# Moving a 2 MB weight load behind the LN2 transposes and fixing ScalarE's and VectorE's order in a two-branch mixer kernel

## Chip, cores, metric

One core of one Trainium2 chip. The metric is the device time of one execution in microseconds (us). Profile times count from the start of the span; the time of a run is about 1.7 us longer than its span (290.91 for a span of 289.2). "Granted clock" is the share of full TensorE clock that the profile records. The record is a list of stretches at 1.00 or 0.50. The mean granted clock also counts a drop in the last microseconds, after the last matmul (from 287.92 in the kernel before).

## The reference

For x of 2048 x 640 (bf16), the output is g * a + (1 - g) * b. Here a is a linear-attention block, g a sigmoid gate per row, and b an MLP with token shifts:

```python
h   = gelu(layernorm(x) @ w1)                  # LN1, W1
hs  = shifted(h) @ w2                          # four column groups, shifted by 1, -1, 2, -2 tokens
x1  = x + hs                                   # W2 and residual
h2  = gelu(layernorm(x1) @ w3) @ w4            # LN2, W3 (640x1728), W4 (1728x640)
b   = x1 + h2
```

## The kernel before

The rows are worked in 4 tiles of 512 rows, each of 4 chunks (`cc`) of 128. TensorE (PE) needs the normalised rows transposed. So ScalarE (ACT) writes a normalised chunk into an `ln` buffer, of which there are three, and a DMA issued on the SP queue transposes it from there into `lnxT`. PSUM is four pairs of banks (`pair()`): a PE unit can start only when an earlier reader has emptied a pair. PE works its units in program order. ScalarE's and VectorE's (DVE) orders are fixed up to the end of W1 tile 1 and left to a scheduler after that.

```python
work = ctx.enter_context(tc.tile_pool(name="work", bufs=3))        # the ln buffers
ps = ctx.enter_context(tc.tile_pool(name="ps", bufs=4, space=PSUM))
# ... cut ...
    def ln1_apply(t, ccs=range(CPT)):
        # ... cut ...
            lnx = work.tile([P, D], BF16, name="ln")
            nc.scalar.activation(lnx[:], x_sb[:, c, :], ACT.Identity, bias=nb1[:, c:c + 1], scale=rstd1[:, c:c + 1])
            nc.sync.dma_start_transpose(lnxT[t][:, :, cc * P:(cc + 1) * P], lnx[:])
# ... cut: end of the first block, whose orders of PE, DVE and ACT are fixed ...
        for fcs in w1_split:
            w1_unit(0, fcs)
        ln1_apply(2)
        for gs in ((0, 1), (2, 3), (4, 5)):
            kv_unit(gs)
        for i, fcs in enumerate(w1_split):
            w1_unit(1, fcs)            # W1 matmuls, then their GELUs on ScalarE
            scale_unit(i)              # a small matmul, then pqT *= PSUM on VectorE
            ln1_apply(3, (i,))
        ln1_apply(3, (3,))

    w4_sb = area.tile([P, FC, D], BF16, tag="a")       # takes the place of the QKV weights
    nc.gpsimd.dma_start(w4_sb[:, 0:FC - 1, :], B_w4[0:(FC - 1) * P, :].rearrange("(c p) f -> p c f", p=P))
    # ... cut: memset and the last 64 rows of w4 ...
    def w2_unit(t, cc):
        # ... cut: 10 matmuls; x1 = PSUM + x and its statistics on VectorE; rstd, nb on POOL ...
        ln = work.tile([P, D], BF16, name="ln")
        nc.scalar.activation(ln[:], x1[:], ACT.Identity, bias=nb[:], scale=rstd[:])
        nc.sync.dma_start_transpose(st[t]["lnT"][:, :, cc * P:(cc + 1) * P], ln[:])
        nc.vector.tensor_scalar_mul(x1[:], x1[:], omg[:, c:c + 1])      # x1 *= 1 - g
# ... cut ...
    with tc.manual_schedule(engines={mybir.EngineType.PE}):
        for cc in range(CPT):
            w2_unit(0, cc)
        for i in range(2 * len(w1_split)):
            w1_unit(2 + i // 3, w1_split[i % 3])
            scale_unit(3 + i)
        scale_unit(9)
        for t in range(NT):
            # ... cut: W3, the next tile's W2, m_unit for t == 0, then W4 ...
```

## Time and profile before

| | before |
|---|---|
| timed runs, median | 293.77 us (292.96 to 294.78) |
| the profiled run: time, span | 290.91 us, 289.2 us |
| PE busy | 272.0 us, 94% of the span |
| mean granted clock | 0.980 |
| PE holes over 1.5 us | 7.87 us and 2.46 us |

From the page of the kernel before: busy tenths of PE and granted clock in 40 slices of 7.2 us.

```profile
span 289.2 us, 4297 instructions
...
PE   6999999999993596999999999999999999999994
...
PEclk9999999999999589999999999999999999999999
```

PE is full except in slices 13, 14 and 16 (and the first and last), and the clock is low in slices 14 and 15. The question is thus what PE waits for there. The table of PE's waits (us in total, times, longest):

```profile
PE pp L348 <- ACT hsT L390: 10.3, 2, 7.9
```

The timeline (start, duration, engine, line, operation; in brackets the idle time before and what ended it) shows the first hole from ScalarE's side:

```profile
83.40 1.38 POOL L448 DMA_DIRECT2D w_sb<-in_B_w_dram  x1 [4.82 <-ACT ln L373]
...
85.75 0.92 ACT L373 ACTIVATE ln<-x_sb,nb,rstd 128x640 bf16<-128x640 bf16 x1 [1.06 <-DMA lnxT<-ln]
...
95.45 0.92 ACT L373 ACTIVATE ln<-x_sb,nb,rstd 128x640 bf16<-128x640 bf16 x1 [8.30 <-DMA lnxT<-ln]
96.27 1.07 ACT L390 ACTIVATE hsT<-pp 128x512 bf16<-128x512 f32 x2
...
97.39 0.61 PE L348 MATMUL pp<-r_bf,emat 32*128 32x512 bf16 x2 [7.87 <-ACT hsT L390]
```

POOL issues the w4 load at 83.40. ScalarE's LN1 of tile 3 (L373 at 95.45) then waits 8.30 us for an `ln` buffer, which a transpose still holds. Behind it in ScalarE's order stands a GELU (L390), and behind that PE's scale matmul (L348). The DMA issues of the window 83 to 98 us (KB each, median us from issue to landing) say why the transposes are late:

```profile
w_sb<-in_B_w_dram POOLq DMA_DIRECT2D x1, 2080.0 KB, 11.4
lnxT<-ln SPq DMA_TRANSPOSE x5, 10.2
```

And PE's own timeline of this stretch, with the second hole:

```profile
97.93 8.37 PE L465 MATMUL pp<-w_sb,hsT 128*128 128x320 bf16 x40
...
115.12 0.39 PE L348 MATMUL pp<-r_bf,emat 32*128 32x512 bf16 x2 [2.46 <-ACT hsT L390]
...
117.03 2.33 PE L382 MATMUL pp<-lnxT,w_sb 128*128 128x512 bf16 x10
...
122.21 2.33 PE L490 MATMUL pp<-lnxT,w_sb 128*128 128x512 bf16 x10
```

W2 of tile 0 (L465, 40 matmuls) takes 8.37 us; elsewhere ten such take about 1.36 us, so 5.4 us would do. The granted clock is why. These are windows of 1 us (window, length, busy us of PE, PEld, DVE, ACT, POOL, granted clock, DMA share, GB/s):

```profile
92.00:93.00 1.00, 0.00 (x0) 0.00 (x0) 0.00 (x0) 0.00 (x0) 0.00 (x0) 1.00 1.15 140
93.00:94.00 1.00, 0.00 (x0) 0.00 (x0) 0.00 (x0) 0.00 (x0) 0.00 (x0) 0.68 1.06 194
...
103.00:104.00 1.00, 1.00 (x7) 0.64 (x6) 0.52 (x1) 0.00 (x0) 0.00 (x0) 0.70 0.27 52
104.00:105.00 1.00, 1.00 (x9) 0.73 (x8) 1.00 (x4) 0.00 (x0) 0.32 (x2) 1.00 0.00 0
```

PE stops at 89.52. The trace's clock record gives half clock from 93.36, thus 3.84 us later (the prediction read about 3.5 from these windows), and full clock again from 103.60.

### The profile page before, as it was taken

The page shows a single profiled execution, that of the slowest core. Times are in us where ns is not written, and L with a number is a line of the kernel's source. Part 1 is how long each engine was busy: PE and PEld are TensorE (multiplying, and loading weights), DVE is VectorE, ACT ScalarE, POOL GpSimd, SP SyncE. Part 2 cuts the span into 40 slices and gives each one's busy share as a digit, 9 for nine tenths or more (in the row PEclk, how much of TensorE's full clock was granted, in tenths as well). Part 3 has the DMA queues.
Part 4 walks back from the last instruction along what each step waited for, and adds up shares of the span by engine and source line. Part 5 has one row for each costly group of instructions (what it writes and reads, how often), then busy time and mean ns, then how long its engine had stood idle before and what let it go on. Part 6 is the DMA issues. An engine that isn't in the chain of part 4 may idle for free.

```text
span 289.2 us, 4297 instructions
## 1 busy us (share of the span) xinstructions
PE 272.0 (94%) x1740; PEld 161.6 (56%) x1740; DVE 131.7 (46%) x261; ACT 98.0 (34%) x121; POOL 37.9 (13%) x95
## 2 busy tenths in 40 slices
PE   6999999999993596999999999999999999999994
PEld 3776444667451252355467755477655577545773
DVE  1798777996954277856105136032244033100121
ACT  1455445244770716435521025411044401144000
POOL 8501000042230023011101002101012010000000
PEclk9999999999999589999999999999999999999999
DMA  7999870219329522102101101101002201100001
GB/s 231 219 306 357 217 297 0 39 31 133 66 41 308 98 57 56 23 2 45 24 2 44 48 23 32 38 22 46 25 23 45 25 24 48 45 0 2 23 25 44
DMA packets 41563, 22.66 MB, mean 78 GB/s; under 512 B 32406, under 2 KB 40471, under 8 KB 41543
## 3 DMA queue, kind: packets, MB, share of 16 engines
q1 hardware_dynamic: 40391, 19.36, 27.2%
q0 software_dynamic: 464, 2.21, 2.5%
q10 hardware_dynamic: 688, 0.82, 0.8%
q8 instruction: 13, 0.21, 0.3%
q14 instruction: 7, 0.06, 0.1%
HBM read 11.96 MB, written 2.62 MB: 50 GB/s over the span
## 4 chain that ended last, share of the span: by engine, by line
PE 82%; DMA 5%; ACT 4%; DVE 4%; POOL 3%; issue 1%; DVEq 0%; SPq 0%; ACTq 0%; POOLq 0%
PE pp L503 21%; PE pp L490 18%; PE pp L297 8%; PE pp L209 8%; PE pp L500 8%; PE pp L222 7%; PE pp L465 6%; DMA lnxT<-ln 4%; PE pp L382 3%; ACT ln L479 2%; POOL rstd L173 1%; DMA x_sb<-in_A_x_dram 1%; DVE x L469 1%; ACT ln L373 1%; PE pp L385 1%
## 5 line engine op out<-in xcount | busy, mean ns | idle before, releaser
L503 PE MATMUL pp<-w_sb,h 128*128 128x320 bf16 x448 | 66.1, 299 | 0.0
L490 PE MATMUL pp<-lnxT,w_sb 128*128 128x512 bf16 x280 | 63.2, 379 | 0.0
L503 PEld LDWEIGHTS <-h 128*128 128x128 bf16 x448 | 43.8, 98 | 17.0
L508 DVE SCALAR_TENSOR_TENSOR oc<-pp,omg,x 128x640 bf16<-128x640 f32 x15 | 13.2, 882 | 80.9 <-PE pp L503 80.9
L492 ACT ACTIVATE h<-pp 128x1024 bf16<-128x1024 f32 x28 | 28.6, 1021 | 61.7 <-PE pp L490 61.7
L490 PEld LDWEIGHTS <-w_sb 128*128 128x128 bf16 x280 | 27.2, 98 | 30.6 <-issue 0.2
L479 ACT ACTIVATE ln<-x,nb,rstd 128x640 bf16<-128x640 f32 x16 | 14.7, 920 | 47.1 <-POOL nb L477 47.1
L184 ACT ACTIVATE e<-pp 128x640 bf16<-128x640 f32 (+2 forms) x28 | 21.7, 779 | 23.5 <-PE pp L209 13.9
L172 POOL TENSOR_SCALAR rstd<-mv 128x1 f32<-128x1 f32 (+1 forms) x20 | 4.5, 226 | 174.3 <-DVE mv L179 166.7
L500 PE MATMUL pp<-m_sb,pqT 128*128 128x320 bf16 x160 | 27.0, 299 | 0.0
L465 PE MATMUL pp<-w_sb,hsT 128*128 128x320 bf16 x160 | 26.6, 322 | 0.0
L209 PE MATMUL pp<-wkq,xT 128*128 128x320 bf16 x160 | 22.4, 299 | 0.3 <-DVE xT L200 0.3
L465 PEld LDWEIGHTS <-hsT 128*128 128x128 bf16 x160 | 16.6, 104 | 10.1 <-issue 0.4
L297 PE MATMUL pp<-pk,x_sb 128*128 128x320 bf16 x160 | 22.1, 299 | 0.0
L222 PE MATMUL pp<-xT,wkq 128*128 128x512 bf16 x100 | 21.9, 379 | 0.0
L469 DVE TENSOR_TENSOR x<-pp,x_sb 128x640 f32<-128x640 f32 x16 | 13.1, 822 | 13.9 <-PE pp L465 13.8
L500 PEld LDWEIGHTS <-pqT 128*128 128x128 bf16 x160 | 15.7, 98 | 6.7
L481 DVE TENSOR_SCALAR x<-x,omg 128x640 f32<-128x640 f32 x16 | 8.8, 553 | 23.0 <-ACT ln L479 22.8
L297 PEld LDWEIGHTS <-x_sb 128*128 128x128 bf16 x160 | 15.6, 98 | 6.4 <-issue 0.3
L373 ACT ACTIVATE ln<-x_sb,nb,rstd 128x640 bf16<-128x640 bf16 x16 | 14.1, 917 | 14.8 <-DMA lnxT<-ln 14.3
L209 PEld LDWEIGHTS <-xT 128*128 128x128 bf16 x160 | 15.4, 98 | 6.5 <-DVE xT L200 0.6
L382 PE MATMUL pp<-lnxT,w_sb 128*128 128x512 bf16 x80 | 18.4, 379 | 0.4 <-ACT hx L393 0.4
(85 smaller groups left out, 209.1 us busy)
## 6 DMA issues: line engine op xcount, KB each, us to landing
out_dram<-oc SPq DMA_DIRECT2D x15, 160.0 KB, 1.8
w_sb<-in_B_w_dram SPq DMA_DIRECT2D x1, 2160.0 KB, 8.9
w_sb<-in_B_w_dram POOLq DMA_DIRECT2D x1, 2080.0 KB, 11.4
x_sb<-in_A_x_dram SPq DMA_DIRECT2D x3, 640.0 KB, 7.2
wkq<-in_A_wqkv_dram SPq DMA_DIRECT2D x2, 800.0 KB, 8.7
w_sb<-in_B_w_dram SPq DMA_DIRECT2D x1, 800.0 KB, 9.8
wo_sb<-in_A_wo_dram SPq DMA_DIRECT2D x5, 150.0 KB, 8.5
wkq<-in_A_wqkv_dram ACTq DMA_DIRECT2D x2, 320.0 KB, 4.5
```

The source lines that it names most:

```text
L184: nc.scalar.activation(ev, src, ACT.Exp)
L209: nc.tensor.matmul(pt[:, hf, 0:HD], lhsT=xT[:, dc, c * P:(c + 1) * P], rhs=wk_sb[:, dc, hf * HD:(hf + 1) * HD], start=(dc == 0), stop=(dc ...
L222: nc.tensor.matmul(pt[:, i, :], lhsT=wq_sb[:, dc, j * P:(j + 1) * P], rhs=xT[:, dc, ts_], start=(dc == 0), stop=(dc == DC - 1))
L297: nc.tensor.matmul(pt[:, hf, 0:HD], lhsT=x_sb[:, c, fc * P:(fc + 1) * P], rhs=pk[:, c, hf * HD:(hf + 1) * HD], start=(c == 0), stop=(c == ...
L373: nc.scalar.activation(lnx[:], x_sb[:, c, :], ACT.Identity, bias=nb1[:, c:c + 1], scale=rstd1[:, c:c + 1])
L382: nc.tensor.matmul(pt[:, i, :], lhsT=w1_sb[:, dc, CG * fc:CG * fc + P], rhs=lnxT[t][:, dc, :], start=(dc == 0), stop=(dc == DC - 1))
L465: nc.tensor.matmul(pt[:, hf, 0:HD], lhsT=hsT[:, fc, 2 + c * P:2 + (c + 1) * P], rhs=w2_sb[:, fc, hf * HD:(hf + 1) * HD], start=(fc == 0), ...
L479: nc.scalar.activation(ln[:], x1[:], ACT.Identity, bias=nb[:], scale=rstd[:])
L490: nc.tensor.matmul(pt[:, i, :], lhsT=w3_sb[:, dc, fc * P:(fc + 1) * P], rhs=lnT[:, dc, :], start=(dc == 0), stop=(dc == DC - 1))
L492: nc.scalar.activation(h2[:, fcs[0]:fcs[-1] + 1, :], pt[:], ACT.Gelu_apprx_tanh)
L500: nc.tensor.matmul(pt[:, hf, 0:HD], lhsT=pqT[:, j, c * P:(c + 1) * P], rhs=m_sb[:, j, hf * HD:(hf + 1) * HD], start=(j == 0), stop=False)
L503: nc.tensor.matmul(pt[:, hf, 0:HD], lhsT=h2[:, fc, cc * P:(cc + 1) * P], rhs=w4_sb[:, fc, hf * HD:(hf + 1) * HD], start=False, stop=(fc == ...
```

## The change

Intent: keep the w4 load out of the way of the transposes, since w4 is first used some 25 us after W3 starts; and keep ScalarE and VectorE in an order that serves PE through W2 of tile 0 and W1 of tiles 2 and 3.

```diff
-    w4_sb = area.tile([P, FC, D], BF16, tag="a")
-    nc.gpsimd.dma_start(w4_sb[:, 0:FC - 1, :], B_w4[0:(FC - 1) * P, :].rearrange("(c p) f -> p c f", p=P))
-    nc.gpsimd.memset(w4_sb[FR:P, FC - 1, :], 0.0)
-    nc.gpsimd.dma_start(w4_sb[0:FR, FC - 1, :], B_w4[(FC - 1) * P:F, :])
 # ... cut: w2_unit now ends with the POOL operations; the rest of it becomes ...
+    def ln2_apply(t, cc):
+        # ... cut ...
         ln = work.tile([P, D], BF16, name="ln")
         nc.scalar.activation(ln[:], x1[:], ACT.Identity, bias=nb[:], scale=rstd[:])
-        nc.sync.dma_start_transpose(st[t]["lnT"][:, :, cc * P:(cc + 1) * P], ln[:])
+        st[t]["dma"] = nc.sync.dma_start_transpose(st[t]["lnT"][:, :, cc * P:(cc + 1) * P], ln[:])
         nc.vector.tensor_scalar_mul(x1[:], x1[:], omg[:, c:c + 1])
 # ... cut ...
-    with tc.manual_schedule(engines={mybir.EngineType.PE}):
+    with tc.manual_schedule(engines=fixed):                 # PE, VectorE, ScalarE
         for cc in range(CPT):
             w2_unit(0, cc)
+        ln2_apply(0, 0)
+        ln2_apply(0, 1)
         for i in range(2 * len(w1_split)):
             w1_unit(2 + i // 3, w1_split[i % 3])
+            if i < 2:
+                ln2_apply(0, 2 + i)
             scale_unit(3 + i)
         scale_unit(9)
+
+    w4_sb = area.tile([P, FC, D], BF16, tag="a")
+    nc.gpsimd.memset(w4_sb[FR:P, FC - 1, :], 0.0)
+    with tc.manual_schedule(engines={mybir.EngineType.PE}):
         for t in range(NT):
             for i, fcs in enumerate(w3_split):
                 w3_unit(t, fcs)
+                if t == 0 and i == 0:
+                    with tc.issue_after(st[0]["dma"].ins):
+                        nc.sync.dma_start(w4_sb[:, 0:FC - 1, :], ...)
+                        nc.sync.dma_start(w4_sb[0:FR, FC - 1, :], ...)
```

`issue_after` fixes only the place in the SP queue; it is not a wait for the transpose to finish.

## The prediction

> **What bounds the kernel.** TensorE: PE is busy 272.0 of a 289.2 us span and 82% of the chain that ended last. The list of PE waits has only two large ones, both where this change acts: a 7.87 us hole (89.5 to 97.4 us) before a scale matmul of W1 tile 1, and one of 2.46 us (112.7 to 115.1) in W1 of tile 2, both "<- ACT hsT". The first has a tail: in 1 us windows the granted clock falls to 0.50 at 93 us and is 1.00 again only at 104. W2 of tile 0 (40 matmuls of 128x320) took 8.37 us there; elsewhere ten such take 1.36 us, so 2.9 us were lost. The Trainium skill ("TensorE: Matmul & The Clock Gate", Part 1) says that an idle window of about 3.4 us halves the clock; this trace agrees (about 3.5 us from stop to drop). Removable in all: 7.9 + 2.9 + 2.5 = 13.3 us.
>
> **Hole 1.** The timeline has the 2 MB w4 load issued from POOL at 83.4, landing 11.4 us later, while the transposes of LN1 tile 2 are in flight: one lands after 11.0 us instead of 2.6. They hold the three ln buffers, so ScalarE's LN1 of tile 3 waits 8.30 us "<- DMA lnxT<-ln", the GELUs of W1 tile 1 stand behind it in ScalarE's order, and PE waits for their PSUM. The skill ("DMA: Bandwidth & Descriptors", "Issuing engines are not separate DMA queues") says that all loads share the same 16 DMA engines; the 11.0 us agrees.
>
> **Hole 2.** The scheduler put LN2 (cc 2) before the GELU on ScalarE and x1*omg between the residual adds on VectorE; LN2 ran at 3 us a chunk (105.9, 108.9, 112.0) and the GELU came at 112.8.
>
> **What the change does.** No work is added or removed. w4 goes to the SP queue behind the last LN2 transpose of tile 0; its first use is some 25 us after W3 starts. VectorE does four times add + statistics (about 2.0 us each) first, x1*omg after; ScalarE two LN2, then GELU and LN2 in turn.
>
> **Replay of the new order with the trace's durations** (estimate). Transposes land in 2.6 us: LN1 (3,0) at 87.2, GELU (0,1) of tile 1 to 89.2, scale at 89.5 (no hole), W2 of tile 0 at full clock 89.9 to 95.4. Then VectorE limits: scale to 92.0, four adds and statistics to 100.1, 2 x 0.55, hx copies 1.2, 0.55, the first scale multiply to 104.1. PE is done with W1 tile 2 at 102.4 and waits about 1.7 us for that PSUM; W3 of tile 0 starts near 111.5 instead of 122.2. Hole 1 and the cold clock (10.8 us) vanish; hole 2 mostly becomes a wait for VectorE. Gain about 10.7 us, all on the critical path, since PE is dense afterwards. w4 is issued near 103 and lands by about 114, 20 us early.
>
> **Prediction: 283.0 us, 280.5 to 286.5; faster by over 2%: 0.94, within 2%: 0.05, slower: 0.01.**
>
> **What would show it.** LN1 transposes near 2.6 us; ScalarE's wait on DMA under 1.5 us; clock 1.00 throughout; W2 of tile 0 about 5.5 us; the largest PE wait 1 to 2.5 us, on VectorE scale multiplies around 102 us; W3 of tile 0 at 110 to 113; everything after as before, shifted.
>
> **What would make it wrong.** Transposes slow for another reason than w4; a VectorE backlog worse than replayed (W3 later than 114, a second clock drop); w4 slowing tile 1's transposes; a wait on w4. If VectorE keeps up fully, 280.5.

## More of the kernel before

The profiled run is 3 us faster than the timed median.

## The result

| | before | after |
|---|---|---|
| timed, median (same rounds) | 293.89 us | 280.18 us (278.43 to 280.47) |
| ratio | | 0.9521, interval 0.9472 to 0.9570 |
| span of the profiled run | 289.2 us | 278.3 us |
| mean granted clock | 0.980 | 1.000 |
| from the first matmul of W1 tile 1 to the first of W3 tile 0 | 82.67 to 122.21: 39.54 us | 84.34 to 111.51: 27.17 us |

A ratio is the mean time of one kernel's runs over that of the other's of the same rounds, so it is not quite the ratio of the medians quoted. The last row of the table, "the stretch" from here on, holds everything that the change touches, and it leaves out what happens at the start. It is used for every experiment below.

The gain is 13.7 us. 10.7 had been forecast, and 280.18 lies below the low end of 280.5. The direction and each cause came out as forecast; two sizes did not.

The page of the changed kernel, in slices of 7.0 us:

```profile
span 278.3 us, 4297 instructions
...
PE   7999999999999989999999999999999999999994
...
PEclk9999999999999999999999999999999999999999
```

PE's waits, those of ScalarE on transposes (80 to 125 us), and the transposes issued between 83 and 98 us:

```profile
PE pp L385 <- DVE pqT L351: 1.1, 1, 1.1
...
PE pp L382 <- ACT hx L393: 0.4, 1, 0.4
```

```profile
ACT ln L373 <- DMA lnxT<-ln: 1.4, 2, 1.1
```

```profile
lnxT<-ln SPq DMA_TRANSPOSE x9, 2.6
```

The 8.30 us wait for a buffer is gone and the transposes land in 2.6 us. The timeline answers to the two holes:

```profile
91.12 0.39 PE L348 MATMUL pp<-r_bf,emat 32*128 32x512 bf16 x2
...
91.44 5.61 PE L460 MATMUL pp<-w_sb,hsT 128*128 128x320 bf16 x40
...
103.48 1.21 DVE L351 TENSOR_TENSOR pqT<-pqT,pp 128x1024 bf16<-128x1024 bf16 x1
...
104.75 1.24 PE L385 MATMUL pp<-lnxT,w1x 128*128 128x512 bf16 x5 [1.14 <-DVE pqT L351]
...
105.05 0.57 SPq L542 DMA_DIRECT2D w_sb<-in_B_w_dram  x1
...
111.51 0.82 PE L491 MATMUL pp<-lnxT,w_sb 128*128 128x512 bf16 x3
```

The scale matmul (L348 at 91.12) waits for nothing, W2 of tile 0 (L460) takes 5.61 us, and what is left is one wait of 1.14 us for a VectorE scale multiplication (L351, done at 104.69). The w4 load is issued at 105.05 on the SP queue.

One warning. W3 of tile 0 starts at 111.51, just where the prediction had it (111.5), but that is chance: this execution came 1.67 us later to W1 of tile 1 than the profiled one of before (84.34 against 82.67). On equal terms W3 starts 1.7 us earlier than forecast.

### The profile page after: what moved, and what is told of

Its sections match the earlier page's. It is cut to its first block, busy times and chain, and to the rows that moved or that the text cites. A ratio compares the mean times of both kernels' runs of the same rounds, so it can differ in the third digit from the quotient of the medians.

```text
span 278.3 us, 4297 instructions
## 1 busy us (share of the span) xinstructions
PE 270.7 (97%) x1740; PEld 161.5 (58%) x1740; DVE 131.3 (47%) x261; ACT 98.2 (35%) x121; POOL 36.1 (13%) x93
## 4 chain that ended last, share of the span: by engine, by line
PE 83%; DVE 8%; ACT 2%; DMA 2%; POOL 1%; issue 1%; DVEq 0%; SPq 0%; POOLq 0%; ACTq 0%
PE pp L504 22%; PE pp L491 19%; PE pp L209 8%; PE pp L297 8%; PE pp L501 8%; PE pp L222 8%; PE pp L460 4%; PE pp L382 3%; DVE x L464 2%; DVE pqT L351 1%; DMA x_sb<-in_A_x_dram 1%; DVE bnst L177 1%; DVE bnst L178 1%; ACT ln L480 1%; DMA lnxT<-ln 1%
## 5 line engine op out<-in xcount | busy, mean ns | idle before, releaser
L460 PE MATMUL pp<-w_sb,hsT 128*128 128x320 bf16 x160 | 23.9, 299 | 0.0
L209 PE MATMUL pp<-wkq,xT 128*128 128x320 bf16 x160 | 23.6, 308 | 0.1
L460 PEld LDWEIGHTS <-hsT 128*128 128x128 bf16 x160 | 15.6, 98 | 8.1 <-issue 0.2
L382 PE MATMUL pp<-lnxT,w_sb 128*128 128x512 bf16 x80 | 18.4, 379 | 0.4 <-ACT hx L393 0.4
L222 PEld LDWEIGHTS <-wkq 128*128 128x128 bf16 x100 | 9.7, 98 | 11.8 <-issue 0.4
## 6 DMA issues: line engine op xcount, KB each, us to landing
wkq<-in_A_wqkv_dram SPq DMA_DIRECT2D x2, 800.0 KB, 10.1
```

Of the source, the lines that this page charges most:

```text
L209: nc.tensor.matmul(pt[:, hf, 0:HD], lhsT=xT[:, dc, c * P:(c + 1) * P], rhs=wk_sb[:, dc, hf * HD:(hf + 1) * HD], start=(dc == 0), stop=(dc ...
L222: nc.tensor.matmul(pt[:, i, :], lhsT=wq_sb[:, dc, j * P:(j + 1) * P], rhs=xT[:, dc, ts_], start=(dc == 0), stop=(dc == DC - 1))
L382: nc.tensor.matmul(pt[:, i, :], lhsT=w1_sb[:, dc, CG * fc:CG * fc + P], rhs=lnxT[t][:, dc, :], start=(dc == 0), stop=(dc == DC - 1))
L460: nc.tensor.matmul(pt[:, hf, 0:HD], lhsT=hsT[:, fc, 2 + c * P:2 + (c + 1) * P], rhs=w2_sb[:, fc, hf * HD:(hf + 1) * HD], start=(fc == 0), ...
```

## The experiments

Theory: (1) w4 made hole 1 and the cold clock behind it; (2) the free orders made hole 2; (3) the miss has two parts, a slower usual state of the kernel before than its profile showed, and a replay of VectorE that was too slow. Rivals stand in each expectation. All fourteen kernels gave correct results. One further edit, six `ln` buffers instead of three, did not fit into SBUF when built.

| run | kernel | timed, us | before in the same job, us | ratio | the stretch, us |
|---|---|---|---|---|---|
| r1 | before, unchanged | 294.50 | 293.64 | 1.0044 | 40.92 |
| r2 | before, w4 late on SP | 283.50 | 293.64 | 0.9664 | 31.17 |
| r3 | after, w4 at its old place | 289.44 | 293.64 | 0.9871 | 36.93 |
| r4 | after, w4 late but on POOL | 283.76 | 293.64 | 0.9680 | 29.71 |
| r5 | before, hole 1 filled with matmuls | 291.08 | 294.23 | 0.9932 | 38.54 |
| r6 | r2, hole 2 filled with matmuls | 282.39 | 294.23 | 0.9618 | 29.49 |
| r7 | r3, GELUs of tile 1 before LN1 of tile 3 | 283.76 | 294.23 | 0.9675 | 30.28 |
| r8 | after, w4 early on SP | 283.60 | 294.23 | 0.9654 | 29.27 |
| r9 | after, unchanged | 280.60 | 294.10 | 0.9533 | 27.16 |
| r10 | after, x1*(1-g) of tile 0 moved back | 279.14 | 294.10 | 0.9480 | 25.89 |
| r11 | after, VectorE's order free | 280.90 | 294.10 | 0.9553 | 27.83 |
| r12 | after, ScalarE's order free | 279.17 | 294.10 | 0.9503 | 27.48 |
| r13 | r10 with two matmuls at the start | 279.56 | 293.48 | 0.9541 | 26.79 |
| r14 | before with two matmuls at the start | 291.90 | 293.48 | 0.9941 | 40.36 |

### r1: the kernel before, once more

No edit.

> The kernel before, unchanged, as a second look at its profile. Its first profiled execution had a span of 289.2 us and a run time of 290.9, while its timed runs take 293 to 295; the changed kernel's profiled and timed runs agree. Theory A (the hole before W2 of tile 0 varies from run to run with how the w4 load and the transposes interleave, and the first profile caught a short one): this profile shows a hole in W1 of tile 1 longer than 7.9 us by 1 to 3 us, with the span longer by as much. Rival B (the difference is a cold start of 1.6 us in the first 10 us, which comes and goes in any kernel): the hole is again 7.9 us within 0.3 and the first 10 us are longer by 1.6. Both may be true; the two parts are read separately.

The hole is 7.82 us again, so theory A falls. Rival B holds for the start, but it is not all of it: in this execution the clock also drops a second time, after the 2.46 us hole. PE's timeline:

```profile
99.15 0.61 PE L348 MATMUL pp<-r_bf,emat 32*128 32x512 bf16 x2 [7.82 <-ACT hsT L390]
99.69 8.02 PE L465 MATMUL pp<-w_sb,hsT 128*128 128x320 bf16 x40
...
116.67 0.39 PE L348 MATMUL pp<-r_bf,emat 32*128 32x512 bf16 x2 [2.46 <-ACT hsT L390]
...
118.79 3.76 PE L382 MATMUL pp<-lnxT,w_sb 128*128 128x512 bf16 x10
...
122.80 2.33 PE L382 MATMUL pp<-lnxT,w_sb 128*128 128x512 bf16 x10
```

The first W1 pair of tile 3 (L382 at 118.79) takes 3.76 us instead of the 2.33 us of the next one. The granted clock in windows of 1 us agrees:

```profile
117.00:118.00 1.00, 1.00 (x7) 0.40 (x5) 1.00 (x2) 0.59 (x2) 0.00 (x0) 1.00 0.69 136
118.00:119.00 1.00, 0.99 (x5) 0.30 (x4) 1.00 (x2) 0.60 (x1) 0.00 (x0) 0.65 0.14 28
119.00:120.00 1.00, 1.00 (x3) 0.30 (x2) 1.00 (x2) 0.00 (x0) 0.00 (x0) 0.50 0.00 0
...
122.00:123.00 1.00, 1.00 (x6) 0.26 (x5) 0.09 (x1) 0.42 (x1) 0.00 (x0) 1.00 0.00 0
```

The first profile had no such drop (its matmuls at 117.03 took 2.33 us). The stretch is 40.92 here and 39.54 there, 1.4 us more; the slowed matmuls account for it (3.76 against 2.33 us and 0.60 against 0.39 make 1.6, W2 of tile 0 is 0.35 shorter). It is the usual state. Five profiles of this record have a hole 2 of 2.46 or 2.51 us: the first one, r1, r2, r5 and r14. In four of them half clock follows it, for 3.41 us each time; only in the first it does not. Of the 32 executions of the kernel before that list a clock in the jobs of r1, r5, r9 and r13 (r1's own four among them), 25 have a mean granted clock of 0.976 or 0.977 and a mean span of 292.3 us. Seven have 0.980 to the third digit and a mean span of 291.1; the profile that the prediction read is among them. By estimate from the records of r1, its two drops (10.24 and 3.41 us) make 0.977. A mean of 0.980 or more is no proof that the second is missing, as r14 shows below.

The start also differs. The matmuls of K in the first 9 us (count, busy us, mean ns) are, before and then in r1:

```profile
L209 PE MATMUL pp<-wkq,xT 128*128 128x320 bf16 x20 | 3.2, 300 | 0.3 <-DVE xT L200 0.3
```

```profile
L209 PE MATMUL pp<-wkq,xT 128*128 128x320 bf16 x8 | 2.5, 471 | 0.1
```

At 471 instead of 300 ns each they run as if the clock were half, although the windows show 1.00 there. That 1.00 is no measurement: the first clock record of r1 begins at 9.07 us and that of the first profile at 4.61, just where the matmuls become fast, and the time before it is counted as full. The changed kernel's profiles begin it at 9.11 and 10.20 (r9). By its spans (278.3, 278.6, 278.8 and 276.7) it probably does both too, but no profile of it with a warm start was kept.

### r2: only the w4 load moved

```diff
-    nc.gpsimd.dma_start(w4_sb[:, 0:FC - 1, :], ...)          # at its old place, on POOL
+                    with tc.issue_after(st[0]["dma"].ins):    # in W3 of tile 0, as in the change
+                        nc.sync.dma_start(w4_sb[:, 0:FC - 1, :], ...)
```

The instructions of PE, VectorE and ScalarE stand in the order of before.

> The kernel before with the w4 load alone moved behind the last LN2 transpose of tile 0, on the SP queue; the orders of PE, VectorE and ScalarE stay those of before. If the collision of w4 with the LN1 transposes makes the long hole and the cold clock: the hole of 7.9 us and the drop of the clock to 0.50 go, the shorter hole in W1 of tile 2 (2.5 us) stays, at 2 to 3 us, and the time is 281.5 to 283, ratio 0.957 to 0.963. Rival (the fixed order does most of it): over 290 us, the long hole is still there.

283.50 us and a ratio of 0.9664, slightly worse than the ranges given (283 and 0.963), since hole 2 brings a clock drop here too. Hole 1 and its cold clock are gone, and hole 2 stands alone:

```profile
PE pp L348 <- ACT hsT L390: 2.5, 1, 2.5
```

In two of four executions the mean clock is 0.994 (spans 282.7 and 282.1), in the other two 0.998 (281.3 and 281.5). So w4 alone is worth 10.1 us.

### r3: only the orders

The changed kernel with the four old lines of w4 put back.

> The changed kernel with the w4 load back at its old place on the POOL queue; only the orders are new. If w4 makes the long hole: LN1 transposes of 8 to 11 us, the hole of about 8 to 10 us and the cold clock are there, the shorter hole is 1 to 1.5 us or gone, and the time is 291 to 293.5, ratio 0.99 to 1.00. Rival (the order does most of it): under 285 us.

289.44 us: more gain than expected (4.2 us), because hole 2 takes its own clock drop along, which the expectation still left out. Hole 1 is what it was, and the transposes of that window land in 10.1 us (median):

```profile
PE pp L348 <- ACT hsT L390: 7.8, 1, 7.8
```

10.1 and 4.2 us add up to 14.3; the whole change gave 13.7. The parts are nearly independent.

### r4: the late load on POOL

```diff
-                    with tc.issue_after(st[0]["dma"].ins):
-                        nc.sync.dma_start(w4_sb[:, 0:FC - 1, :], ...)
+                    with tc.issue_after(st[0]["nbi"].ins):    # nb of the last chunk of tile 0, on POOL
+                        nc.gpsimd.dma_start(w4_sb[:, 0:FC - 1, :], ...)
```

> The changed kernel with the late w4 load issued from POOL, behind the LN2 bias of the last chunk of tile 0, about 1 us earlier than from SP. If the time of the load is what counts: 279.5 to 281, as the changed kernel; the last LN2 transpose of tile 0 may land late, but it has some 5 us of slack. Rival (what hurt was the POOL queue itself[...]): the last LN2 transpose lands after 8 us or more, and if the slack is used up W3 of tile 0 starts late and the time is 283 or more.

283.76 us: the theory's number fails, although the load came late. It is issued at 101.10, one microsecond ahead of the last LN2 transpose. Transposes issued before it (window 99 to 101.9) and the one behind it (101.9 to 104); the last figure is us to landing:

```profile
lnxT<-ln SPq DMA_TRANSPOSE x2, 2.6
```

```profile
lnxT<-ln SPq DMA_TRANSPOSE x1, 10.1
```

W3 needs that transpose, and PE waits for it:

```profile
112.39 3.27 PE L491 MATMUL pp<-lnxT,w_sb 128*128 128x512 bf16 x10 [2.42 <-DVE pqT L351]
```

The record names VectorE's scale multiplication, which ended at nearly the same moment. But with the same order of instructions the changed kernel starts W3 before those multiplications begin (111.51 against 111.61), and here the transpose, issued at about 102.1, landed 10.1 us later at 112.2. The wait is 2.42 us and brings a cold clock of its own (3.27 us instead of 2.33 for ten matmuls). What protects the transposes in the changed kernel is thus the place behind the last of them, not merely a later time. Whether POOL's queue is worse in itself this run can't say; r8 bears on it.

### r5: hole 1 filled with needless matmuls

```diff
     def w1_unit(t, fcs, warm=0):
         pt = pair()
+        for i in range(warm):
+            nc.tensor.matmul(pt[:, i % 2, :], lhsT=ident[:], rhs=r_bf[:], start=True, stop=True)
 # ... cut ...
-            w1_unit(1, fcs)
+            w1_unit(1, fcs, warm=34 if i == 2 else 0)
```

> The kernel before with 34 needless 128x512 matmuls (7.7 us at 227 ns each) put into the long hole: PE does them in the PSUM pair of the third W1 unit of tile 1 just before its real matmuls. The hole is thus filled, and the clock should not fall. If the cold clock after the hole costs 2.6 to 2.9 us by itself: W2 of tile 0 takes 5.5 to 5.6 us instead of 8.0 to 8.4, and the time falls by 2 to 3 us against before although PE does 7.7 us more work: 290.5 to 292, ratio 0.990 to 0.994. Rival (slow W2 matmuls come from the DMA traffic or from waits, not from the clock): W2 still takes 8 us and the time is not below before's.

PE fills the hole (one record of the 34 is missing) and then does W2 of tile 0 (L467) in 5.61 us:

```profile
88.92 7.50 PE L380 MATMUL pp<-r_bf,ident 128*128 128x512 bf16 x33 [0.37 <-ACT hx L395]
...
99.47 5.61 PE L467 MATMUL pp<-w_sb,hsT 128*128 128x320 bf16 x40
```

The transposes are as late as before and the DMA traffic is the same, so the slow W2 was the clock and nothing else. The time falls by 3.1 us though PE does 7.7 us more work; over three rounds its interval (0.9856 to 1.0009) does not exclude no change, so the claim rests on the 5.61 against 8.02 to 8.37 us.

### r6: hole 2 filled

The same edit on r2, with 10 needless matmuls in the third W1 unit of tile 2.

> The kernel with only the w4 load moved, and 10 needless 128x512 matmuls (2.3 us) put into the shorter hole in W1 of tile 2, in the PSUM pair of the third W1 unit of tile 2 before its real matmuls. If the shorter hole drops the clock in some executions, as the profiles with granted clocks of 0.994 and W1 matmuls of tile 3 at 3.8 instead of 2.3 us suggest: mean granted clock 1.000 in every run here, no stretched W1 matmuls, and about 1 to 1.5 us less than the kernel with only w4 moved wherever that had 0.994: 281.5 to 282.8 (its own 283.5), if the GELU of that unit is not pushed later by more than the hole. Rival (0.994 has another source): clocks of 0.994 in some runs as before.

282.39 us, 1.1 below r2. The two are of different jobs, and the intervals of the ratios overlap (0.9554 to 0.9682 and 0.9601 to 0.9727), so the gain itself is not shown. No W1 group is stretched in the profile; the clocks are 0.997, 1.000, 1.000 and 0.998 instead of 0.994 and 0.998. The 0.997 of the profiled execution has nothing to do with hole 2: its only half clock is in the last 1.6 us of the span (from 279.11), after the last matmul (277.02). So no drop follows the filled hole here. A wait of 0.91 us stays ahead of the filling.

### r7: another cure for hole 1

```diff
             scale_unit(i)
-            ln1_apply(3, (i,))
-        ln1_apply(3, (3,))
+        ln1_apply(3)
```

on r3, so w4 collides as before.

> The kernel with only the orders changed (w4 at its old place on the POOL queue, colliding as before) and ScalarE's four LN1 of tile 3 moved behind all GELUs of W1 tile 1. If the collision hurts through ScalarE's order (GELUs standing behind an LN1 that waits for a transpose): the transposes still land after 8 to 11 us, ScalarE still waits 7 us or more for them, but the PE hole of 7.8 us shrinks below 4 us since W2 of tile 0 can run, and the time falls from 289.4 to 282 to 286. Rival (PE needs the late transposes themselves): the hole keeps its size and the time stays at 289 to 290.

ScalarE's waits on transposes (80 to 125 us) and PE's largest:

```profile
ACT ln L373 <- DMA lnxT<-ln: 6.8, 4, 4.8
```

```profile
PE pp L385 <- DVE mv L179: 2.2, 1, 2.2
PE pp L348 <- ACT hx L393: 1.8, 1, 1.8
```

ScalarE still waits 6.8 us for the late transposes, slightly under the 7 expected, but PE's 7.8 us hole is now two of 2.2 and 1.8 us, and the time is 283.76. The collision reached PE through ScalarE's order: a GELU that was ready stood behind an LN1 whose buffer was not.

### r8: early, on the SP queue

The changed kernel with w4 behind `ln1_dma[2]`, the last LN1 transpose of tile 2, and ahead of those of tile 3.

> The changed kernel with the w4 load on the SP queue but early, behind the LN1 transposes of tile 2 and before those of tile 3. If a load on the SP queue spares the transposes issued before it and holds up only those behind it[...]: LN1 transposes of tile 2 land in 2.6 to 5 us, those of tile 3 in 7 to 11, the hole before W2 of tile 0 is gone, a later one of 1 to 4 us comes when ScalarE waits for an ln buffer of tile 3, and the time is 281 to 285. Rival (only the time of the load counts, not the queue): a hole of 7 to 8 us before W2 of tile 0 as before, 288 to 290.

283.60 us, as expected. The transposes ahead of the load (issued 83 to 90.3) and behind it (91 to 97):

```profile
lnxT<-ln SPq DMA_TRANSPOSE x4, 2.6
```

```profile
lnxT<-ln SPq DMA_TRANSPOSE x2, 7.9
```

Ahead of the load they land in 2.6 us (the last of them in 3.8). Of the two behind, whose median this is, the first took 8.8 us and the second 6.9. A third, issued at 97.40, took 5.0. Behind a load on POOL it was 11.0, 10.2 and 6.8 us in before and 10.1 in r4. Counted from the issue of the load, the three land after 10.2 to 12.0 us here and after 11.9 to 13.0 in before. So a transpose issued behind the load is late on either queue; one run of each does not show that POOL's queue is worse in itself. ScalarE waits 6.78 us for a buffer of tile 3, and PE's longest wait is 2.85 us. The SP queue is of use to the change because the transposes are issued there, so the load can be placed behind one without a wait.

### r9 to r12: what is left, and what made hole 2

r9 is the changed kernel unchanged. r10:

```diff
-        nc.vector.tensor_scalar_mul(x1[:], x1[:], omg[:, c:c + 1])       # in ln2_apply
+        if t > 0:
+            omg_mul(t, cc)
 # ... cut: omg_mul holds that line ...
         scale_unit(9)
+        for cc in range(CPT):
+            omg_mul(0, cc)
```

r11 and r12 change one set each:

```diff
-    with tc.manual_schedule(engines=fixed):
+    with tc.manual_schedule(engines={PE, Activation}):     # r11; r12 has {PE, DVE}
```

> The changed kernel, unchanged, as the reference for the next three on the same chip: 279.5 to 281, ratio 0.950 to 0.957. Mean granted clock 1.00 in every execution. Its spans fall into two groups about 1.6 us apart (cold or warm matmuls in the first 9 us); the executions of the kernel before do the same, so this cancels in the ratio.

280.60 us, clock 1.000 in all four executions.

> The changed kernel with the four multiplications of x1 of tile 0 by 1-g (0.5 us each on VectorE) moved behind the last scale multiplication. If the remaining PE wait of 1.1 us is VectorE's backlog: that wait goes or falls below 0.3 us, W3 of tile 0 starts 0.8 to 1.2 us earlier relative to W1 of tile 1, and the time is 0.6 to 1.2 us below the changed kernel of this job. Rival (PE would wait there anyway, for ScalarE): the same time within 0.3 us.

279.14 us, 1.46 below r9; the ratios are 0.9480 and 0.9533, and their intervals touch only at the edge (0.9513 and 0.9512). W1 of tile 3 (L385) no longer waits:

```profile
103.35 1.25 PE L385 MATMUL pp<-lnxT,w1x 128*128 128x512 bf16 x5
...
110.03 2.33 PE L497 MATMUL pp<-lnxT,w_sb 128*128 128x512 bf16 x10
```

The stretch is 25.89 against 27.16 us. So the last wait was VectorE's backlog, and four multiplications of 0.55 us that nobody needed yet were enough to make it.

> The changed kernel with VectorE's order left to the scheduler (ScalarE's stays fixed): VectorE again has x1*(1-g) between the residual adds, as before. If ScalarE's order alone (a GELU behind an LN2) made the 2.5 us hole: the time stays within 0.7 us of the changed kernel. If VectorE's order made it (the 3 us per chunk of LN2): a hole of 1.5 to 2.5 us in W1 of tile 2 stays, with a chance of the cold clock, and the time is 2 to 3.5 us above the changed kernel, close to the run with only w4 moved (283.5).

> The changed kernel with ScalarE's order left to the scheduler (VectorE's stays fixed): ScalarE has both last LN2 of tile 0 ahead of the GELUs of W1 tile 2. If VectorE's order made the 2.5 us hole: at most 0.5 to 1 us more than the changed kernel. If ScalarE's order did: a hole of 1.5 us or more before a scale matmul or the next W1 unit, and 1.5 to 3 us above the changed kernel.

r11 takes 280.90 and r12 279.17 us, both within noise of r9. The stretch, which leaves out the start, is 27.83 and 27.48 us, thus 0.7 and 0.3 us longer than r9's. Each expectation offered one engine as the culprit. Either fixed order alone shrinks hole 2 (the longest waits are 0.9 and 1.5 us), and with both free (r2) it is 2.51. But r11 is not the test that it was meant to be: left free, VectorE did not fall back into the order of before. It finished the second chunk's statistics (L179 at 97.36) ahead of the first x1*(1-g) (98.32), where r2 has them (99.26) behind it (98.79). LN2 ran at 97.36, 99.03, 102.07 and 103.85; in r2 it ran at 97.84, 100.84, 103.99 and 105.66. So the old order of VectorE was never run with the new one of ScalarE. In r12 ScalarE had both last LN2 ahead of the GELUs, as expected, and that leaves a wait of 1.50 us. How the 2.46 us divide between the two engines stays open.

### r13 and r14: the cold start

```diff
         xT_unit(0, 1)
+        warm_unit(2)
         xT_unit(1, 1)
```

on r10 (r13) and on before (r14).

> The changed kernel with the multiplications by 1-g moved back, and two more needless 128x512 matmuls between the first two input transposes, where PE idles about 0.6 to 1 us for the second block of x. If the spread of 1.6 us between executions is the clock still at half in the first 9 us, and the small hole there is what decides it: the first K matmuls run at 300 ns instead of 471 in the profile, the executions fall into the faster group alone, and the time is 277.3 to 278.3 (1 to 1.6 us below the kernel with only the multiplications moved, 279.1). Rival (the start waits on data, not on the clock): no change, or 0.3 us worse.

> The kernel before with the same two needless matmuls at the start. If the cold start explains part of why its timed runs (293.9) are slower than its first profiled one (290.9), and a clock drop after the 2.5 us hole the rest: the cold start goes, the time falls by 1 to 1.6 us to 292.3 to 293, the mean granted clock stays at 0.976 to 0.980 and W1 matmuls of tile 3 are stretched in executions with 0.976 or 0.977 alone. Rival (the spread lies elsewhere): 294 as before.

In r14 the first matmuls warm up sooner than in r1 (first clock record at 6.29 against 9.07 us) and the time falls to 291.90 us, 1.6 below before, ratio 0.9941 (0.9907 to 0.9974). One part of its expectation failed: stretched W1 matmuls were to come with a clock of 0.976 or 0.977 alone. All four executions have 0.981 or 0.982, and yet the profiled one has them:

```profile
115.34 2.19 PE L385 MATMUL pp<-lnxT,w1x 128*128 128x512 bf16 x5
...
118.00 2.77 PE L382 MATMUL pp<-lnxT,w_sb 128*128 128x512 bf16 x10
```

Unslowed they take 1.25 and 2.33 us. The mean is higher because the first drop lasted 6.83 us here instead of 10.24: hole 1 came in two parts (2.14 and 6.44 us), and W2 of tile 0 took 7.06. So the mean clock alone does not tell which drops an execution had. And the gain need not be all from the start: against r1, W1 of tile 1 is reached 1.22 us earlier (83.25 and 84.47), and the stretch is 0.56 us shorter.

In r13 the profile starts warm (4.73 us), as those of before, r3, r4 and r12 did without the edit, but the time, 279.56 us, is not below r10's, ratio 0.9541 against 0.9480: one of four executions shows a clock of 0.994, and the profile has a wait of 0.81 us before a scale matmul that r10 had not. So the gain at the start shows in one kernel and not in the other, and that stays open. The cold start strikes both kernels, so it is not what the prediction missed. The lowest time is r10's; r12 and r13 lie within noise of it.

## Why the prediction was wrong

- **What bounds the kernel, and hole 1: right.** r2 and r3 part the change. The transposes fall from 10.2 to 2.6 us, ScalarE's longest wait from 8.30 to 1.1, W2 of tile 0 from 8.37 to 5.61. r5 shows the clock part alone, r7 the way through ScalarE's order.
- **Hole 2: right in kind.** The free orders of ScalarE and VectorE made it (2.51 us with both free in r2, 1.14 with both fixed, on another engine); each engine's share stays open (r11, r12).
- **The step that failed first: "Removable in all: 7.9 + 2.9 + 2.5 = 13.3 us".** The clock term, 2.9, covers the drop after hole 1 only. Hole 2 also drops the clock in most executions (four of five profiles): 1.4 us by the stretch of r1 (40.92 - 39.54). The profiled run happened to lack it; that was bad luck. The sign of it was at hand: 290.91 us profiled and 293.77 timed. The gain was read in the one and subtracted from the other.
- **The second: the replay, "waits about 1.7 us for that PSUM; W3 of tile 0 starts near 111.5".** From W1 of tile 1 the replay makes 111.5 - 82.67 = 28.8 us, measured 27.17. VectorE was taken at 2.0 us a chunk and does four in a row at about 1.87 (adds at 93.47, 95.36, 97.22, 99.07), so its first scale multiplication ends at 104.69 - 1.67 = 103.0 instead of 104.1. And PE needs 6.76 us from there to W3 (104.75 to 111.51) instead of 7.4. The records of its groups add up to 7.06, since each starts a little before the record of the one ahead of it ends; adding durations thus explains 0.3 of the 0.6, and the rest is not shown. 1.1 + 0.6 = 1.7 us.
- **The sum.** 10.7 + 1.4 + 1.7 = 13.8 us, against 13.7 measured. So close a fit is partly chance: the interval of the ratio alone is worth 1.4 us either way.
- **Placing of w4: right.** It is issued at 105.05, 103.4 on the clock of before, and PE has no wait on it. What the prediction had as a single term, "behind the last LN2 transpose", matters to the microsecond: issued one microsecond ahead of that transpose (r4, from POOL) it costs 3 us.

The Trainium skill had the warning. "TensorE: Matmul & The Clock Gate", Part 1, says that the activity window is free-running and that the same kernel therefore meets it differently from run to run. The prediction took the 3.4 us from that section and counted a clock loss only where one profile showed it. The runs agree with the free-running window: in every kept trace the stretches of the clock record between its first and last change are multiples of 3.41 us (3.41, 6.83, 10.24, 13.65 and so on). On this grid hole 2 of the first profile falls into two intervals, 1.17 and 1.30 us in each, and no drop follows. In r1, r2, r5 and r14, 1.77 to 2.46 us of it fall into one interval, and the clock drops at its end. Idle time alone does not settle it: in r8 an interval with 1.93 us of idle PE was followed by no drop. "DMA: Bandwidth & Descriptors", "Issuing engines are not separate DMA queues", agrees with r4 and r8.

## What to carry to other kernels

Before a gain is read off a profile, compare the profiled run with the timed ones. Where they differ by more than the noise, profile the kernel again and look at the clock over time behind each hole; the mean granted clock of every run is a hint, but r14 shows that it can hide a drop. A hole that is too short for a drop in one execution may have one in the next. Place a large load by what stands behind it in the queue: a transfer needed soon must be issued before it, and in r4 a microsecond decided. An engine that is far from busy (VectorE, 47%) can still hold up PE for a stretch; move what nobody needs yet, like the four multiplications of r10, behind what PE waits for.

## What the Trainium skill lacked or had wrong

- "TensorE: Matmul & The Clock Gate", "Why this matters for your kernels", gives about 3 us as the idle gap to stay under. Here a hole of 2.46 us was followed by half clock (0.50 in the window from 119 to 120 us of r1, costing 1.4 us), in four of five profiles with such a hole (2.46 or 2.51 us), and 25 of 32 executions of that kernel have the lower mean clock. By the mean clock, no drop followed the 1.1 us wait in any of the eight listed executions of the changed kernel (r9 and the first four, all at 1.000).
- The same page describes the cold start, but no page says how the time before the first clock record is to be read. Here it is the cold time: the first record begins at 9.07 us in r1 and at 4.61 in before, and until 9 us the matmuls of 128x320 take 471 ns in r1 instead of 300, while the windows count 1.00.
- "DMA: Bandwidth & Descriptors" says that all issuing engines share the same 16 DMA engines. No page gives the cost for a small transpose issued behind a 2 MB load: the first one behind it took 11.0 (before) and 10.1 us (r4) with the load on another queue and 8.8 on the same one (r8), instead of 2.6.
